# Attention-pack and channel mix on one core: first sequence's table and shares in long runs, v in two transfers, second sequence held, and a new order of all parts

## The chip, the cores and the metric

The kernel runs on one core of one Trainium2 chip. The metric is the device time in microseconds (us) of one execution. Several executions are timed, and their median is given; one further execution is profiled.

A core has TensorE (PE, matrix products), VectorE (DVE), ScalarE (ACT), GpSimd (POOL), and SyncE (SP), which here only starts transfers. DMA engines move data between device memory and on-chip memory; a transfer is started by an instruction on one engine's queue.

## The reference, cut to what matters

```python
def sm_attn(qq, kk, vv):                       # 8 sequences, 8 heads, 576 tokens, head size 64
    s = scale * np.matmul(qq, kk.transpose(0, 1, 3, 2))
    s = s - np.max(s, axis=-1, keepdims=True)
    a = np.exp(s)
    a = a / (np.sum(a, axis=-1, keepdims=True) + 1e-09)
    return np.matmul(a, vv)
p_packed = sm_attn(p, k, v)                    # p: 32 rows for each head
x = sm_attn(q, p_packed, p_packed)             # then heads side by side: 8 x 576 x 512

x_prev = shifted by one token within the sequence, zero ahead of the first
xk = mu_k * x + (1.0 - mu_k) * x_prev
xr = mu_r * x + (1.0 - mu_r) * x_prev
k = np.maximum(xk @ w_k, 0.0)                  # 512 -> 1024
v = k * k @ w_v                                # 1024 -> 512
r = 1.0 / (1.0 + np.exp(-(xr @ w_r)))          # the gates, 512 -> 512
out = r * v
```

## The kernel before, in words

**The two halves.** The attention half is called a front; there is one per sequence (b = 0 to 7). It multiplies k by p (L441 for the first sequence, L601 for the others), takes a softmax over the tokens, turns the weights (L687, L688), multiplies them by v (L462 or L623), and so has the packed rows. Then q meets the packed rows (L496 or L749), a second softmax over 32 follows, and the packed rows are mixed (L839 in the first sequence, where the mixing by mu_k, mu_r and the shift by one token are folded into the product with the shares `mub`; L796 and the DVE and ACT lines L916 to L936 in the others).

The first sequence's front is special: it goes in two sides, h = 0 and h = 1, of four heads each, and each step has its instructions once per side (`first_side`).

The second half works on 9 blocks of 512 tokens of all sequences side by side: gates (xr by w_r, L998 to L1000 for the first block, L1020 to L1022 later), keys (xk by w_k, L953 to L955, squared on ACT and DVE) and values (squared keys by w_v, L1049 to L1051). Each weight is held as a high and a low part in a reduced format, so each product of the second half is three matmuls. The last four blocks are computed in pairs with fewer products (L1353).

**The weights.** `convert` makes the two parts of each 128 x 512 piece of a weight from 64-bit numbers: a transfer into `st`, one ACT instruction (L344, `m` from one half of `st`), one shift on DVE (L350), one DVE instruction that joins in the other half (L352), a cast on ACT to the high part (L356) and a subtraction on DVE (L358). It has a second way, `by_act`, in which ACT runs one more instruction in place and DVE one in place of two; a piece takes it while fewer than RANK_LATE13 pieces have been begun. With 0.991 none does.

**The order.** `Flow` is a planner that runs when the program is built. All work is written as parts (generators), each with a rank; a part names its engine and its estimated time, waits for events, and takes and gives back buffer slots. The planner keeps a clock for each engine and always issues the instruction that can start first, ties broken by rank. What it issues is the fixed program order on each engine. On the chip the engines then run that order and wait for each other by semaphores; the planner's times play no part there. Where its clock shows TensorE idle, it issues `fill` (L1681): a product of the identity with itself that nothing reads. `fronts` starts the two sides of sequence 0 and then the other fronts one after the other.

**The first transfers.** SP starts k, v, q and the weights. p of the first sequence and the shares by channel (`mus`) go by ACT's queue, and the shares `mub` of the first sequence by POOL's:

```python
for hh, half in enumerate(HALVES):
    yield from load(pt[half, :, hh], p[0, half].rearrange("p (r n) -> p r n", n=NP), 0.5, 0.1, "scalar")
```

`pt` is cleared by POOL first; the two transfers write runs of 32 numbers (128 bytes). `mub` is spread over 64 partitions by 8 transfers of 64 x 128 numbers. v of one half sequence comes by one transfer of 512 KB (runs of 4 KB) and one small one.

Of the kernel before, what the change touches and what calls it, by code (L numbers as in the profile page):

```python
# [17 lines left out]
class Flow:  # L18
# [13 lines left out]
    URGENT = 10.6  # L32
# [158 lines left out]
def attn_pack_channel_mix(ctx: ExitStack, tc: tile.TileContext, q, k, v, p, mu_k, mu_r, mu_by_channel, w_k, w_v, w_r, out):  # L191
# [22 lines left out]
    FIRST = 19.125, 23.858, 15.496, 14.378  # L214
    RANK_1, RANK_MIX, RANK_KEYS, RANK_R, RANK_W, RANK_W2, RANK_V, LOADS_1, RANK_SQ, RANK_REST, HOLD_V, HOLD_S = 14.138, 6.204, 10.067, 22.577, 16.168, 18.235, 23.505, 24.159, 0.05, -0.644, 0.056, 0.212
    RANK_LATE1 = -1.892
    RANK_LATE2 = 4.895
    RANK_LATE3 = 0.077
    RANK_LATE4 = 7.126
    RANK_LATE5 = 4.101  # L220
    RANK_LATE6 = 1.945
    RANK_LATE13 = 0.991
    RANK_LATE12 = 22
# [29 lines left out]
    LANDS = 2.0  # L253
    MARGIN = 0.8
# [3 lines left out]
    def reached():  # L258
# [13 lines left out]
                pa=2, both=1, m=4, n=4, staged=4, ex=3, pair=0, ring=0, store=2, twin=0)  # L272
# [48 lines left out]
    def convert(w, hi, lo, c, o, n, event, first=None):  # L321
# [7 lines left out]
        yield from load(st[:, :2 * n], w[c * P:(c + 1) * P, o:o + n].bitcast(U32), 0.46, 3.5e-3 * n)  # L329
# [41 lines left out]
    def turned(src, tag, b, pr):  # L371

        slot = yield from flow.take("kq")
        t = tile_([P, S], F32, "kq", slot, tag)
        yield from load(t, src[b, pr], 0.46, 1.0)
        ts[tag, b, pr] = slot, t
        flow.set((tag, b, pr))
# [22 lines left out]
    def values_of(b, h):  # L400
# [7 lines left out]
        yield from load(vt[HALVES[h] if b >= MOVED else HALVES[0], 4], rest, 0.46, 0.3)  # L408
# [11 lines left out]
    def first_packed():  # L420
# [123 lines left out]
    def first_constants():  # L544
# [14 lines left out]
        for h in range(2):  # L559
            t = tile_([P, 4, P], F32, "sig", firsts["mu", h], "mub")  # L560
# [1187 lines left out]
```

## Time and profile before

| | before |
|---|---|
| timed runs, us | 561.14, 563.05, 563.52; median 563.05 |
| profiled execution, us | 561.01 |
| its span in the trace, us | 558.9 |
| TensorE busy | 550.4 us, 98% of the span |
| VectorE busy | 430.1 us, 77% |
| ScalarE busy | 349.0 us, 62% |
| moved by DMA | 86.10 MB, mean 154 GB/s |

The span is what the trace covers; 2.1 us of the profiled execution lie around it. TensorE's busy time includes the fills (L1681), so 98% doesn't say that 98% is work. A matmul's own duration overlaps the next one's: where the stream is dense, 512-column matmuls last about 0.39 us each and start about 0.227 us apart. So stretches are measured from start to start here.

### The profile page before, as it was taken

The numbers are of one execution on the slowest core, as the hardware profiler recorded it, in microseconds if no ns is written. First come the engines' busy times: TensorE is split into PE (matmuls) and PEld (weight loads), VectorE is DVE, ScalarE is ACT, GpSimd is POOL, SyncE is SP. The second block draws the span as 40 slices with busy tenths as digits, with TensorE's granted clock in tenths as the row PEclk, the third lists the DMA queues.
The fourth block names the chain that finished last, engine by engine and source line by source line (L and its number), as shares of the span: only waits on it lengthen the run. The fifth ranks groups of instructions, "written<-read, shape, count | busy, mean of one in ns | idle before, by whom it ended". The sixth has DMA issues, their size and how long they took to land.

```text
span 558.9 us, 9836 instructions
## 1 busy us (share of the span) xinstructions
PE 550.4 (98%) x3623; PEld 430.5 (77%) x3623; DVE 430.1 (77%) x857; ACT 349.0 (62%) x664; POOL 7.2 (1%) x36
## 2 busy tenths in 40 slices
PE   7999999999999999999999999999999999999997
PEld 6865787777777777777777877788888888888885
DVE  1788896878798599876798589924399894879863
ACT  2467776666675279356565468747797647877650
POOL 4000000000000000000000000000000000000000
PEclk9999999999999999999999999999999999999999
DMA  8985943445736563674614420220361480634242
GB/s 265 401 276 167 362 136 99 155 139 164 226 110 220 173 230 93 210 257 140 209 61 179 133 95 1 79 73 1 103 198 42 148 263 1 199 103 149 65 145 94
DMA packets 57135, 86.10 MB, mean 154 GB/s; under 512 B 6272, under 2 KB 33024, under 8 KB 57088
## 3 DMA queue, kind: packets, MB, share of 16 engines
q1 hardware_dynamic: 55424, 84.17, 45.4%
q10 hardware_dynamic: 1408, 1.05, 0.6%
q8 instruction: 28, 0.46, 0.3%
q0 software_dynamic: 256, 0.26, 0.2%
q14 instruction: 19, 0.16, 0.1%
HBM read 62.00 MB, written 23.46 MB: 153 GB/s over the span
## 4 chain that ended last, share of the span: by engine, by line
PE 83%; DVE 11%; ACT 2%; issue 2%; DMA 1%; DVEq 0%; ACTq 0%
PE ph L1353 31%; PE pvo L1049 6%; PE ph L953 6%; PE pvo L1050 5%; PE pvo L1051 5%; PE ph L954 5%; PE ph L955 5%; PE pr L1020 3%; PE pr L1021 3%; PE pr L1022 3%; PE pa L796 2%; PE pa L623 1%; DVE m L352 1%; PE pr L1509 1%; PE pr L1511 1%
## 5 line engine op out<-in xcount | busy, mean ns | idle before, releaser
L953 PE MATMUL ph<-xk,wk_h 128*128 128x512 f32 x160 | 64.1, 401 | 0.0
L1049 PE MATMUL pvo<-wv_h,sq 128*128 128x512 f32 x160 | 63.9, 399 | 0.2 <-ACT r L965 0.2
L954 PE MATMUL ph<-xk,wk_h 128*128 128x512 f32 x160 | 62.4, 390 | 0.0
L1050 PE MATMUL pvo<-wv_l,sq 128*128 128x512 f32 x160 | 62.4, 390 | 0.0
L955 PE MATMUL ph<-xk,wk_l 128*128 128x512 f32 x160 | 62.3, 389 | 0.0
L1051 PE MATMUL pvo<-wv_h,sq 128*128 128x512 f32 x160 | 62.2, 389 | 0.0
L965 ACT ACTIVATE r<-ph 128x512 f32<-128x512 f32 x40 | 23.9, 598 | 39.5 <-PE ph L955 29.8
L1353 PE MATMUL ph<-vT,ring 128*128 128x512 f32 x156 | 38.7, 393 | 0.0
L1049 PEld LDWEIGHTS pvo<-wv_h,sq 128*128 128x128 f32 x160 | 30.0, 188 | 11.3 <-issue 4.5
L953 PEld LDWEIGHTS ph<-xk,wk_h 128*128 128x128 f32 x160 | 30.0, 188 | 10.5 <-issue 4.1
L920 DVE SCALAR_TENSOR_TENSOR x<-xt,mus,x 128x64 f32<-128x64 f32 (+5 forms) x80 | 34.9, 480 | 4.1 <-ACT x L916 4.1
L916 ACT ACTIVATE x<-xt,mus 128x64 f32<-128x64 f32 (+5 forms) x80 | 35.8, 501 | 3.1 <-DVE xr L936 1.2
L955 PEld LDWEIGHTS ph<-xk,wk_l 128*128 128x128 f32 x160 | 30.0, 188 | 6.4
L1051 PEld LDWEIGHTS pvo<-wv_h,sq 128*128 128x128 f32 x160 | 30.0, 188 | 6.4
L1353 PE MATMUL ph<-vB,wv_h 128*128 128x512 f32 x112 | 34.8, 392 | 0.0
L1050 PEld LDWEIGHTS pvo<-wv_l,sq 128*128 128x128 f32 x160 | 30.1, 188 | 5.7
L954 PEld LDWEIGHTS ph<-xk,wk_h 128*128 128x128 f32 x160 | 30.1, 188 | 5.7
L1353 PEld LDWEIGHTS ph<-vT,ring 128*128 128x128 f32 x156 | 29.3, 188 | 6.6
L920 DVE SCALAR_TENSOR_TENSOR chain<-xt,mus,chain 128x448 f32<-128x448 f32 (+6 forms) x40 | 20.4, 535 | 17.3 <-ACT chain L916 17.1
L1031 ACT ACTIVATE sig<-pr 128x512 f32<-128x512 f32 x28 | 16.4, 600 | 21.5 <-PE pr L1022 11.3
L972 DVE CAST sq<-r 128x512 fp32r<-128x512 f32 x40 | 16.6, 417 | 16.2 <-ACT r L968 15.3
L974 DVE TENSOR_TENSOR sq<-r,sq 128x512 fp32r<-128x512 f32 x40 | 27.2, 683 | 0.2
(209 smaller groups left out, 1301.5 us busy)
## 6 DMA issues: line engine op xcount, KB each, us to landing
sum<-sw SPq DMA_DIRECT2D x40, 256.0 KB, 2.3
kT<-in_k SPq DMA_DIRECT2D x32, 288.0 KB, 4.5
qT<-in_q SPq DMA_DIRECT2D x32, 288.0 KB, 4.9
ring<-sum SPq DMA_DIRECT2D x36, 256.0 KB, 3.8
vt<-in_v SPq DMA_DIRECT2D x16, 512.0 KB, 5.7
out<-sig SPq DMA_DIRECT2D x32, 256.0 KB, 3.5
wv_h<-sum SPq DMA_DIRECT2D x18, 256.0 KB, 3.4
wv_l<-sum SPq DMA_DIRECT2D x18, 256.0 KB, 3.9
```

What stands on the lines that cost most here:

```text
L916: nc.scalar.mul(x32[:, o:o + n], xts[b, c][:, 1 + s:1 + s + n], mus[:, j, c:c + 1])
L920: nc.vector.scalar_tensor_tensor(x32[:, o:o + n], xts[b, c][:, s:s + n], mus[:, j + 1, c:c + 1], x32[:, o:o + n], op0=ALU.mult, op1=ALU.add,)
L953: nc.tensor.matmul(ph, wk_h[:, c, fs], xh, start=(c == 0), stop=False)
L954: nc.tensor.matmul(ph, wk_h[:, c, fs], xl, start=False, stop=False)
L955: nc.tensor.matmul(ph, wk_l[:, c, fs], xh, start=False, stop=(c == NC - 1))
L965: nc.scalar.activation(r, ph, AF.Relu)
L974: nc.vector.tensor_tensor(hl[:, 1, :], r, hl[:, 0, :].bitcast(F32), op=ALU.subtract)
L1020: nc.tensor.matmul(pr, xh[:, ts_], wr_h[:, c, :], start=(c == 0), stop=False)
L1049: nc.tensor.matmul(pv[t], sh, wv_h[:, f, :], start=(n == 0), stop=False)
L1050: nc.tensor.matmul(pv[t], sh, wv_l[:, f, :], start=False, stop=False)
L1051: nc.tensor.matmul(pv[t], sl, wv_h[:, f, :], start=False, stop=(n == NF - 1))
L1353: nc.tensor.matmul(bank[2], w, x, start=(not more and step == k == 0), stop=(step == 2 and k == count - 1), skip_group_check=True,)
```

## The change: what it does

1. p of sequence 0 is laid out on the host with its zeros (`p_first`), and comes in one transfer with runs of 1 KB on ACT's queue. POOL's clearing of `pt` goes.
2. The shares of the first sequence are spread over the partitions on the host (`mu_first`), and come in two transfers with runs of 1 KB on ACT's queue. The 8 POOL transfers go. `mus` comes in one transfer in place of two, and is now the first on ACT's queue.
3. The large part of v comes in two transfers with runs of 2 KB in place of one with runs of 4 KB, for every half sequence (16 more transfers on SP).
4. `fronts` waits until both sides of sequence 0 are mixed before it begins sequence 1.
5. All ranks, the planner's estimates for transfers, and two of its limits are new. RANK_LATE13 is 8.231, so the first 8 weight pieces take the way `by_act`.

Line numbers move: L441 to L529 stay; in what follows L839 is now L835, L687 is L683, L601 is L597, L998 is L994, L953 is L949, L1681 is L1675.

```diff
-    FIRST = 19.125, 23.858, 15.496, 14.378
...
-    RANK_LATE13 = 0.991
-    RANK_LATE12 = 22
+    FIRST = 8.643, 12.628, 9.429, 21.798
...
+    RANK_LATE13 = 8.231
+    RANK_LATE12 = 0.668
...
-        begin = max(flow.free.get("dma", 0.0), flow.t + 0.46)
+        begin = max(flow.free.get("dma", 0.0), flow.t + 0.46, SLOW[0])
+        if begin < SLOW[1]:
+            us *= SLOW[2]
...
+    SLOW = 1.2, 8.0, 1.3
...
-        yield from load(vt[:, :4], main, 0.46, 1.8)
-        back_to_issue()
+        for c in range(0, 4, 2):
+            yield from load(vt[:, c:c + 2], main[:, c:c + 2], 0.46, 0.65)
+            back_to_issue()
...
-        nc.gpsimd.memset(pt, 0.0)
-        for hh, half in enumerate(HALVES):
-            yield from load(pt[half, :, hh], p[0, half].rearrange("p (r n) -> p r n", n=NP), 0.5, 0.1, "scalar")
-            if not hh:
-                back_to_issue("scalar")
+        yield from load(pt, p_first.rearrange("p (r a n) -> p r a n", a=2, n=NP), 0.5, 0.25, "scalar")
...
-            t = tile_([P, 4, P], F32, "sig", firsts["mu", h], "mub")
-            for j, mu in ((2, mu_r), (0, mu_k)):
-                for c in range(2):
-                    at = (2 * h + c) * P
-                    yield from load(
-                        t[64 * c:64 * c + 64, j], mu[at:at + P].unsqueeze(0).broadcast_to([64, P]), 1.0, 0.02, "gpsimd"
-                    )
-                    back_to_issue("gpsimd")
+            t = tile_([P, 2, 2, P], F32, "sig", firsts["mu", h], "mub")
+            yield from load(t[:, 0], mu_first[:, h], 0.5, 0.3, "scalar")
+            back_to_issue("scalar")
...
         flow.spawn(rest_of_first(), RANK_REST)
+        yield from flow.wait(*(("mixed", h, tag) for h in range(2) for tag in ("xr", "xk")))
         for b in range(1, B):
...
-        for j in range(2):
-            yield from load(mus[:, 2 * j], mu_by_channel[:, j], 0.46, 0.02, "scalar")
-            if not j:
-                back_to_issue("scalar")
+        yield from load(mus[:, 0::2], mu_by_channel, 0.46, 0.02, "scalar")
```

**Three places in the order.** The first is TensorE at the start of the program, before the change:

```order
L1681 MATMUL spare<-ident 128x128 x12
L441 MATMUL pa<-kT,pt 64x288 x4
L1681 MATMUL spare<-ident 128x128 x10
L687 MATMUL pa<-ident,a 128x128 x4
L688 MATMUL pa<-ident,a 64x128
L1681 MATMUL spare<-ident 128x128 x5
L462 MATMUL pv<-vt,aT 32x64 x20
L1681 MATMUL spare<-ident 128x128 x2
L483 MATMUL pT<-ident,pm 128x128
L441 MATMUL pa<-kT,pt 64x288 x4
L496 MATMUL pa<-both,qT 128x64 x10
```

The same place after the change:

```order
L1675 MATMUL spare<-ident 128x128 x12
L441 MATMUL pa<-kT,pt 64x288 x4
L1675 MATMUL spare<-ident 128x128 x3
L441 MATMUL pa<-kT,pt 64x288 x4
L1675 MATMUL spare<-ident 128x128
L683 MATMUL pa<-ident,a 128x128 x4
L684 MATMUL pa<-ident,a 64x128
L1675 MATMUL spare<-ident 128x128 x5
L462 MATMUL pv<-vt,aT 32x64 x20
L683 MATMUL pa<-ident,a 128x128 x4
L684 MATMUL pa<-ident,a 64x128
L483 MATMUL pT<-ident,pm 128x128
```

The second L441, of side h = 1, stood behind the whole first softmax of h = 0 and its product with v; it now stands 3 fills behind the first L441. The 12 fills at the very start stay. In the whole program there are 62 fills before and 45 after.

The second place is TensorE around the first gates (L998 and L994), before the change, from the mixing of side h = 0 to the scores of sequence 1:

```order
L529 MATMUL pa<-ident,e 128x128
L1681 MATMUL spare<-ident 128x128 x9
L839 MATMUL pa<-a2t,mub 128x512 x4
L1681 MATMUL spare<-ident 128x128 x8
L998 MATMUL pr<-wr_h,xr 128x512
L999 MATMUL pr<-wr_l,xr 128x512
L1000 MATMUL pr<-wr_h,xr 128x512
L601 MATMUL pa<-kT,pt 32x288 x16
```

After the change:

```order
L1675 MATMUL spare<-ident 128x128 x4
L835 MATMUL pa<-a2t,mub 128x512 x4
L1675 MATMUL spare<-ident 128x128 x6
L529 MATMUL pa<-ident,e 128x112 x4
L529 MATMUL pa<-ident,e 128x128
L994 MATMUL pr<-wr_h,xr 128x512
L995 MATMUL pr<-wr_l,xr 128x512
L996 MATMUL pr<-wr_h,xr 128x512
L1675 MATMUL spare<-ident 128x128
L835 MATMUL pa<-a2t,mub 128x512 x4
L994 MATMUL pr<-wr_h,xr 128x512
```

Side h = 1 is turned (L529) ahead of the first gate, and its mixing (L835) comes directly behind it. Before, L529 of h = 1 stood behind 15 gate matmuls, and its L839 behind that. L601 of sequence 1 stood behind the first 3 gate matmuls; as L597 it now stands behind 27, with 21 left before the keys. Sequence 1's L687 (twice), L623, L653 and L749, which stood among the gates, stand as L683, L619, L649 and L745 among the keys of the first block: the first L683 is behind 30 key matmuls.

The third place is ACT around the first weight pieces, before the change (`a` and `e` belong to the softmaxes, `st`, `m` and `wr_h` to `convert`):

```order
L674 ACTIVATE a,sm<-pa,nmx 128x576
L514 ACTIVATE e<-e 128x640
L344 ACTIVATE m<-st 128x512 x2
L486 COPY both<-pT 128x128
L344 ACTIVATE m<-st 128x512
L356 CAST wr_h<-m 128x512
L344 ACTIVATE m<-st 128x512
```

After the change:

```order
L670 ACTIVATE a,sm<-pa,nmx 128x576
L345 ACTIVATE st<-st 128x512
L347 ACTIVATE m<-st 128x512
L486 COPY both<-pT 128x128
L345 ACTIVATE st<-st 128x512
L359 CAST wr_h<-m 128x512
L347 ACTIVATE m<-st 128x512
L514 ACTIVATE e<-e 128x640
L486 COPY both<-pT 128x128
```

L345 is the new ACT instruction, once for each of the first 8 pieces (4 of w_r, 4 of w_k). On DVE the shift (L350 before, L353 after) falls from 20 to 12, and the joining instruction stays at 20. Two pieces are now begun ahead of the second softmax of side h = 0 (L514).

## Rows read from the trace of the kernel before

**Rows 1.** Stretches: length; busy (instructions) PE, PEld, DVE, ACT, POOL; clock; DMA share; GB/s.

```profile
0.00:20.00 20.00, 16.66 (x151) 14.77 (x152) 4.68 (x13) 4.15 (x9) 6.07 (x25) 1.00 0.90 300
20.00:40.00 20.00, 19.88 (x198) 16.27 (x196) 19.12 (x40) 12.31 (x25) 0.00 (x0) 1.00 0.91 334
40.00:60.00 20.00, 18.98 (x187) 11.34 (x187) 15.30 (x30) 16.10 (x33) 0.10 (x1) 1.00 0.60 203
60.00:80.00 20.00, 20.00 (x116) 15.87 (x115) 19.45 (x39) 14.83 (x25) 0.00 (x0) 1.00 0.62 223
...
380.00:400.00 20.00, 20.00 (x89) 16.45 (x88) 10.36 (x18) 17.06 (x33) 0.00 (x0) 1.00 0.08 23
```

**Rows 2.** Timeline of TensorE, 0 to 33 us; at the end idle time before.

```profile
1.59 5.14 PE L1681 MATMUL spare<-ident 128*128 128x128 f32 x24 [1.59 <-POOL ident masks.py:199]
8.48 1.19 PE L441 MATMUL pa<-kT,pt 128*64 128x288 f32 x8 [1.75 <-DMA qT<-in_q]
9.60 2.50 PE L1681 MATMUL spare<-ident 128*128 128x128 f32 x20
...
15.40 1.19 PE L441 MATMUL pa<-kT,pt 128*64 128x288 f32 x8
16.52 2.44 PE L496 MATMUL pa<-both,qT 128*128 128x64 f32 x20
...
23.96 2.44 PE L496 MATMUL pa<-both,qT 128*128 128x64 f32 x20
...
28.84 1.99 PE L839 MATMUL pa<-a2t,mub 64*128 64x512 f32 x8
...
32.57 0.47 PE L998 MATMUL pr<-wr_h,xr 128*128 128x512 f32 x1
```

**Rows 3.** DMA issues of the first 25 us: KB each, median us to landing.

```profile
kT<-in_k SPq DMA_DIRECT2D x8, 288.0 KB, 5.1
...
pt<-in_p ACTq DMA_DIRECT2D x2, 32.0 KB, 6.1
```

**Rows 4.** Groups by line and form, 9 to 60 us: busy us, mean ns.

```profile
L344 ACT ACTIVATE m<-st 128x512 f32<-128x512 f32 x14 | 9.1, 686 | 0.0
...
L350 DVE TENSOR_SCALAR m<-m 128x512 uint32<-128x512 uint32 x13 | 5.4, 414 | 0.5 <-ACT m L344 0.5
L475 DVE SCALAR_TENSOR_TENSOR pm<-pv,rs,both 128x128 f32<-128x128 f32 x2 | 0.7, 348 | 2.8 <-PE pv L462 2.8
L699 DVE COPY aT<-pa 128x512 f32<-128x512 f32 x1 | 0.7, 680 | 0.0
```

**Rows 5.** Timeline of TensorE, 33 to 59 us.

```profile
33.44 1.35 PE L601 MATMUL pa<-kT,pt 64*32 64x288 f32 x32
...
38.26 0.66 PE L529 MATMUL pa<-ident,e 112*128 112x112 f32 x5
...
39.84 0.66 PE L687 MATMUL pa<-ident,a 128*128 128x128 f32 x4
...
40.54 3.70 PE L839 MATMUL pa<-a2t,mub 64*128 64x512 f32 x16
...
45.66 1.99 PE L839 MATMUL pa<-a2t,mub 64*128 64x512 f32 x8 [0.52 <-DVE xr L852]
...
51.21 1.48 PE L623 MATMUL pa<-vt,aT 128*32 128x64 f32 x80 [0.48 <-DVE xk L852]
...
56.61 1.20 PE L749 MATMUL pa<-qT,ppT 64*32 64x288 f32 x32
...
58.54 0.40 PE L953 MATMUL ph<-xk,wk_h 128*128 128x512 f32 x1
```

**Rows 6.** Timeline of TensorE, 93 to 108 us, around the second block's first gate (L1020).

```profile
93.36 0.74 PE L796 MATMUL pa<-a,pm 32*64 32x288 f32 x16
...
107.24 0.39 PE L1020 MATMUL pr<-wr_h,xr 128*128 128x512 f32 x1
```

**Rows 7.** Timeline of VectorE at the same place.

```profile
107.19 0.68 DVE L936 TENSOR_TENSOR xr<-x,xr 128x512 fp32r<-128x512 f32 x1
```

More of the change, by code (lines that the diff above doesn't have):

```diff
@@ L31 @@
     HOLD = {}
-    URGENT = 10.6
+    URGENT = 21.126
     CHANGE = 0.1
@@ L190, in attn_pack_channel_mix @@
 @with_exitstack
-def attn_pack_channel_mix(ctx: ExitStack, tc: tile.TileContext, q, k, v, p, mu_k, mu_r, mu_by_channel, w_k, w_v, w_r, out):
+def attn_pack_channel_mix(ctx: ExitStack, tc: tile.TileContext, q, k, v, p, p_first, mu_first, mu_by_channel, w_k, w_v, w_r, out):
     nc = tc.nc
@@ L211, in attn_pack_channel_mix @@
     flow = Flow()
-    FIRST = 19.125, 23.858, 15.496, 14.378
[L215 to L221, printed above, removed]
-    RANK_LATE13 = 0.991
-    RANK_LATE12 = 22
+    FIRST = 8.643, 12.628, 9.429, 21.798
+    RANK_1, RANK_MIX, RANK_KEYS, RANK_R, RANK_W, RANK_W2, RANK_V, LOADS_1, RANK_SQ, RANK_REST, HOLD_V, HOLD_S = 29.742, 22.85, 24.95, 30, 25.349, 24.645, 30, 29.932, 0.818, -6.71, 0.315, 0.438
+    RANK_LATE1 = -1.079
+    RANK_LATE2 = 0.189
+    RANK_LATE3 = 1.091
+    RANK_LATE4 = 9.432
+    RANK_LATE5 = 9.05
+    RANK_LATE6 = 20.949
+    RANK_LATE13 = 8.231
+    RANK_LATE12 = 0.668
     FIRST_K, FIRST_V, FIRST_Q = (RANK_LATE1, RANK_LATE2), (RANK_LATE3, RANK_LATE4), (RANK_LATE5, RANK_LATE6)
@@ L328, in convert @@
         st = tile_([P, 2 * WP], U32, "sq", slot, "st")
-        yield from load(st[:, :2 * n], w[c * P:(c + 1) * P, o:o + n].bitcast(U32), 0.46, 3.5e-3 * n)
+        yield from load(st[:, :2 * n], w[c * P:(c + 1) * P, o:o + n].bitcast(U32), 0.46, 2.45e-3 * n)
         flow.now.rank = rank
@@ L374, in turned @@
         t = tile_([P, S], F32, "kq", slot, tag)
-        yield from load(t, src[b, pr], 0.46, 1.0)
+        yield from load(t, src[b, pr], 0.46, 0.7)
         ts[tag, b, pr] = slot, t
@@ L724, in weights_moved @@
         away = dram.tile([P, NTB, NP], F32, name="away", tag=f"away{h}")
-        yield from load(away, blocks, 0.5, 0.9)
+        yield from load(away, blocks, 0.46, 0.8)
         flow.give("e", se)
@@ L839, in mixed_on_pe @@
                 nc.tensor.matmul(
-                    px[:, c, :TB], shares_of[half, j + t, :], a2[half, h, 1 - t:1 - t + TB], start=(t == 0), stop=(t == 1),
+                    px[:, c, :TB], shares_of[half, t, j // 2, :], a2[half, h, 1 - t:1 - t + TB], start=(t == 0), stop=(t == 1),
                 )
@@ L1062, in done @@
         t0 = i * TB + t * P
-        yield from load(out[t0:t0 + P, :], sig, 0.63, 0.75)
+        yield from load(out[t0:t0 + P, :], sig, 0.46, 0.65)
         flow.give("sig", sg)
@@ L1191, in stored @@
             yield from reached()
-            yield from load(dst, both, 0.5, 0.9)
+            yield from load(dst, both, 0.46, 0.65)
             flow.give("tmp", slot)
@@ L1250, in arriving @@
         for h, half in enumerate(both):
-            yield from load(half.bitcast(F32), sums[kind, SUM_OF[n], k][:, :, h], 0.5, 0.9)
+            yield from load(half.bitcast(F32), sums[kind, SUM_OF[n], k][:, :, h], 0.46, 0.65)
             if not h:
@@ L1592, in out_of_pair @@
         queue = "scalar" if i == PAIRS[-1] and n in (7, 4) else "queue"
-        yield from load(out[b * TB + d * P:b * TB + (d + 1) * P, :], sig, 0.46, 0.9, queue)
+        yield from load(out[b * TB + d * P:b * TB + (d + 1) * P, :], sig, 0.46, 0.65, queue)
         flow.give("sig", sg)
@@ L1716, in laid_out @@
     x['v'] = np.stack(by_half, axis=1)
-    x['mu_by_channel'] = np.stack([x['moe_mu_k'].reshape(-1, 128).T, x['moe_mu_r'].reshape(-1, 128).T], axis=1)
+    mus = np.stack([x['moe_mu_k'], x['moe_mu_r']]).reshape(2, -1, 128)
+    x['mu_by_channel'] = mus.transpose(2, 0, 1)
+    by_heads = mus.reshape(2, 2, 2, 1, 128).transpose(2, 3, 1, 0, 4)
+    x['mu_first'] = np.broadcast_to(by_heads, (2, 64, 2, 2, 128)).reshape(128, 2, 2, 128)
+    first = np.zeros((2, D, H // 2, 2, n), x['p'].dtype)
+    for h in range(2):
+        first[h, :, :, h] = x['p'][0].reshape(2, D, H // 2, n)[h]
+    x['p_first'] = first.reshape(2 * D, H * n)
     return x
```

15 lines of the change are left out of this document (8 added, 7 removed).

## The prediction

> **What bounds the kernel now.** I read the stretches first, because the busy shares of the whole span hide that the stages have different limits. In a late stretch (380 to 400 us) TensorE is busy all 20.00 us with 89 matmuls, one each 0.225 us: it is the bound, and DVE (10.36) and ACT (17.06) follow it [rows 1]. From 60 us on the stretches look like this one. Ahead of it they don't: to 20 us DVE and ACT are busy under 5 us each while DMA is at 0.90, and between 20 and 40 us DVE is busy 19.12 of 20 [rows 1]. TensorE's busy time there is partly fills and long gaps between products that matter.
>
> Next the timeline of TensorE shows what those first stages wait for. The first real product, L441 of side h = 0, starts at 8.48 behind a named wait of 1.75 us for a transfer [rows 2]. Side h = 1 has its L441 only at 15.40, and its L496 at 23.96, 7.44 behind that of h = 0 [rows 2]. The first gate is at 32.57, 24.1 us after the first L441. The keys begin at 58.54 [rows 5], 25.97 us after the first gate, and from there TensorE's dense stream runs to the end. So this change is worth what it moves the keys' start, less what it moves behind that start, plus what it makes late later.
>
> **The change part by part.**
>
> *p and the first product.* The two transfers of p take a median of 6.1 us from issue to landing although they hold 32 KB each; a kT of 288 KB takes 5.1 [rows 3]. So p's time is not bytes, and 128 runs of 1 KB in place of 512 of 128 bytes should bring it nearer to the kT's, or below. Bounds: no gain, 0; and the most that the fills allow. The 12 fills are 24 rows of the trace, from 1.59 for 5.14 us, and they end at 6.73 [rows 2]; L441 stands behind them in the new order too, and POOL's clearing of `pt`, gone now, stood ahead of the identity that they need, so they may end some tenths sooner. I take 6.4 as the earliest start of L441; the gain is 0 to 2.1. p is now issued behind `mus` on ACT's queue, one issue later than before, so I don't take the whole: **−1.8**, L441 at 6.7.
>
> *From the first L441 to the first gate, 24.1 us before.* In the new order L441 of h = 1 (1.19 us long [rows 2]) no longer stands between the softmax of h = 0 and its L496: −1.1. Between the reductions of the second softmax of h = 0 (L509 to L522), DVE ran a copy of 0.680, two shifts of 0.414 and L475 of 0.348 [rows 4], 1.86 us, and three small ones, some 2.4 in all; now it runs L475, two small ones and one subtraction on 512 columns, as long as the copy, some 1.3 in all: −1.1. The first gate needs this side alone. A further 0.4 is that fewer shifts stand between the mixing L839 and the gate. Sum **−2.6**, first gate at 28.2; bounds −1 (DVE's other work was in its gaps) and −4 (the h = 1 side doesn't collide at all).
>
> *From the first gate to the keys, 25.97 us before.* What TensorE has to do there is now 48 gate matmuls at 0.227, 10.9; L835 three more times at 1.85 to 1.99 [rows 5], 5.8; L597, 1.35 [rows 5]; L864, a product of 65 columns, 0.7 as I estimate it from L529's 0.66 [rows 5]; together 18.8, and 1.4 for changes between kinds of product and one wait as the two of 0.52 and 0.48 at 45.66 and 51.21 [rows 5]: 20.2, keys at 48.4. That is 10.1 earlier than 58.54. But sequence 1's L687 (twice 0.66), L623 (1.48), L749 (1.20) [rows 5], 4.0 in all, only moved behind the keys' start. TensorE's gain at an equal amount of work is therefore 10.1 − 4.0 = 6.1: the 1.8 and 2.6 above and **−1.7** here. Here the bounds are 0 and −2.8: waits as long as before, or none. What used to stall (mixing of h = 1 behind DVE's and ACT's conversions) finds DVE freer: the shifts of 8 pieces, 8 x 0.414 = 3.3 [rows 4], are gone from it.
>
> *by_act.* Those 8 pieces cost ACT 8 x 0.686 = 5.5 us more [rows 4], all in the first 50 us. ACT is busy 12.31 and 16.10 of 20 there [rows 1], so 5.5 fits the sum, but most of what it has free is ahead of 40 us. What waits behind it is the exponential of sequence 1, without which L683 holds TensorE's queue among the keys, and the squares' first step of the keys. Bounds 0 and 3 (half of 5.5); **+0.8**.
>
> *Second sequence held.* L601 was at 33.44, L597 stands 7 gate groups ahead of the keys, at about 42.2. The path from there to the second block's gates was 73.8 us (33.44 to L1020 at 107.24 [rows 5, 6]), and will be 60.7. At the end of it nothing was spare: xr's last subtraction on DVE is at 107.19 and L1020 at 107.24 [rows 6, 7] (it needs that xr only for its last steps). From L796 at 93.36 to this the chain takes 13.8 [rows 6, 7], and the order leaves it about 14.6. Work fits: some 80 DVE instructions lie in the window, at the 0.50 of 60:80 (19.45 for 39 [rows 1]) 40 us of 60.7. **+0.5**, 0 to 1.
>
> *The order of transfers.* kT of h = 1 now comes ahead of the first v, as do shares and two weight pieces ahead of q of h = 1. Up to the q that the second L496 needs, SP's and ACT's orders hold 5.5 MB. Before, 6.0 MB were moved by 20.00 us (300 GB/s [rows 1]), so 5.5 are there at about 18.5 and landed some tenths to 2 us later; I have that L496 at 19.9. **+0.6**, 0 to 1.2. v in halves: 16 more issues on SP, which only issues, and whose transfers from 40 us on leave DMA at a share of 0.60 and less [rows 1]: 0, and if that cover were gone, some 0.5 each time that v is the last to land.
>
> **Sum:** −1.8 − 2.6 − 1.7 + 0.8 + 0.5 + 0.6 = −4.2. The profiled execution took 561.01 (span 558.9 and 2.1 around it), so 556.8. The three timed runs' median stands 2.0 above the profiled one, so the same change would be 558.8 on it; I give **557.5**, between. The bounds together reach from about 552 (−2.1 − 4 − 2.8) to the old time.
>
> *A rule against it.* To 6.7 us TensorE's fills pass at 5.14/24 = 0.214 us each, from 9.60 at 2.50/20 = 0.125 [rows 2]: by that pace TensorE starts at the lower of its two clock levels (1.2 of 2.4 GHz), and had risen after it was kept busy, though the column of the granted clock says 1.00 throughout [rows 1]. The Trainium skill, "TensorE: Matmul & The Clock Gate", section "HAM oscillation — how this bites in real kernels", says that idle gaps put TensorE back to the lower level, so that each next batch starts cold; 45 fills in place of 62 leave more such gaps. By the rows the sum stands as above. By the rule, one fall between 7 and 28 us would double the short products that follow until it has risen, about the 4.6 us of a side's L441, L496 and L687 at half pace, and cost 2.3 more: 559.8. No stretch here shows TensorE slower again once it had risen, with gaps of the same kind among its products [rows 1, 2], so I give it 0.05.
>
> **The rivals.**
>
> *A. Transfers hold it (0.12).* DMA is at 0.90 of its share to 20 us [rows 1], and the same bytes come in. If q and w_r pieces are what h = 1 and the gates wait for, the second and third term shrink to about −1 each, and +1.2 stands for the order: −2.6, about **559.5**. For it: the share. Against it: DVE is busy 19.12 of 20 between 20 and 40 us, with data there [rows 1].
>
> *B. ACT becomes the limit in the first keys (0.14).* The extra 5.5 us come out at the exponential of sequence 1, TensorE stops at L683, and squares come late for the values. Then +3, and with a first product that gains only 1: −1.2, about **561.8**, no change that can be told. For it: 16.10 of 20 already busy in 40:60 [rows 1].
>
> *C. The second sequence is held too long (0.09), slower than before.* DVE's 40 us and the tail of 13.8, taken one behind the other, are 53.8 of the 60.7 us from L597 to L1020, so 6.9 are left for waits between the chain's steps; before, with 73.8, they took 20. As soon as they take over 6.9, TensorE has no other work at L1020 and stops, us by us; if they take three quarters of the old 20, 15, it waits 8, and the time is **565.5**. For it: nothing was spare at 107.24 [rows 6, 7]. Against it: L601 was begun early, and most of the 20 lay where its chain had time.
>
> *D. More than I sum (0.10).* No term later, the first ones near their bounds: **552.5**.
>
> **How the numbers follow.** The forecast has 0.50, the rule 0.05, A 0.12, B 0.14, C 0.09, D 0.10. Within 0.5% (2.8 us, about what a measurement here can tell from no change) of 563.05 lie B and a part of A's and the forecast's upper end. Faster by over 0.5%: 0.73; within: 0.18; slower: 0.09. The range is 552 to 562: it leaves out C and the ends of B and D. The forecast's own range is 555 to 560.
>
> **What would show it.** L441 at 6.4 to 7.5 and its second one right behind; the second L496 within 6 us of the first; the first gate at 27 to 29.5, the first key at 47 to 50; among the first keys no idle time of TensorE ahead of L683 above 1 us; L1020 at 102 to 104.5 with DVE's xr just ahead. A late landing of p or of a first v behind `mus`, an idle TensorE ahead of L683, or ahead of L1020, would make it wrong, each by the size of that gap.

## The result, and the profile after

The changed kernel takes 556.01 us (median of 554.85, 555.34, 556.68, 557.18) against 563.17 for the kernel before, beside which it ran; the ratio is 0.988, with a 95% interval of 0.985 to 0.991. That is faster by about 7 us. 557.5 was predicted, with a range of 552 to 562.

The profiled executions differ by less than the medians (7.16 us): 554.85 against 561.01, which is 6.16, and spans of 553.3 against 558.9, which is 5.6. The 0.55 between these two is time outside the span: 2.1 us before and 1.5 after. What makes that differ isn't shown; it lies between 1.5 and 2.2 in all runs below. So there are two things to find: where the trace's 5.6 come from, and what the medians have beyond them.

The timeline of TensorE after the change, rows that answer to [rows 2], [rows 5] and [rows 6]:

```profile
1.48 5.03 PE L1675 MATMUL spare<-ident 128*128 128x128 f32 x24 [1.48 <-POOL ident masks.py:199]
6.43 1.19 PE L441 MATMUL pa<-kT,pt 128*64 128x288 f32 x8
8.42 1.19 PE L441 MATMUL pa<-kT,pt 128*64 128x288 f32 x8
14.04 2.44 PE L496 MATMUL pa<-both,qT 128*128 128x64 f32 x20
19.59 2.44 PE L496 MATMUL pa<-both,qT 128*128 128x64 f32 x20
23.90 1.99 PE L835 MATMUL pa<-a2t,mub 64*128 64x512 f32 x8
27.67 0.48 PE L994 MATMUL pr<-wr_h,xr 128*128 128x512 f32 x1
...
41.83 1.20 PE L597 MATMUL pa<-kT,pt 64*32 64x288 f32 x32
47.90 0.39 PE L949 MATMUL ph<-xk,wk_h 128*128 128x512 f32 x1
55.96 0.65 PE L683 MATMUL pa<-ident,a 128*128 128x128 f32 x4 [1.10 <-ACT a L670]
101.69 0.40 PE L1016 MATMUL pr<-wr_h,xr 128*128 128x512 f32 x1
```

The reader can lay these starts beside those of before and take differences. L441 is at 6.43 for 8.48 (−2.05). From there to the first gate it is 21.24 us for 24.09 (−2.85), from the gate to the first key 20.23 for 25.97. Of these last 5.74, 4.0 are the work of sequence 1 that moved behind the key, so −1.74. At the key the gain is 6.64. From the key to the second block's gate it is 53.79 for 48.70, 4.0 of which are that work: 1.1 lost, and the row of L683 names it, an idle time of 1.10 ahead of it until ACT's exponential. The gain at L1020, now L1016, is 5.55, and at the end 5.6: behind 102 us the change neither gained nor lost on balance.

The −2.85 between L441 and the first gate are not one thing. These rows of DVE, TensorE and ACT, first before and then after, part them:

```profile
9.72 0.76 DVE L668 TENSOR_REDUCE mx<-pa 128x1 f32<-128x576 f32 x1 [9.72 <-PE pa L441]
19.00 0.82 DVE L509 TENSOR_REDUCE m<-pa 128x20 f32<-128x640 f32 x1 [1.39 <-PE pa L496]
23.42 0.81 DVE L522 TENSOR_TENSOR e<-e,m 128x640 f32<-128x640 f32 x1
26.24 0.67 PE L529 MATMUL pa<-ident,e 112*128 112x112 f32 x5
26.74 2.17 PE L1681 MATMUL spare<-ident 128*128 128x128 f32 x18
27.37 0.27 ACT L536 COPY a2t<-pa 128x128 f32<-128x128 f32 x1
```

```profile
7.96 0.29 DVE L568 TENSOR_SCALAR mub<-mub 128x256 f32<-128x256 f32 x1 [3.75 <-DMA mub<-in_mu_first]
8.17 0.75 DVE L664 TENSOR_REDUCE mx<-pa 128x1 f32<-128x576 f32 x1
16.52 0.83 DVE L509 TENSOR_REDUCE m<-pa 128x20 f32<-128x640 f32 x1 [0.83 <-PE pa L496]
20.62 0.83 DVE L522 TENSOR_TENSOR e<-e,m 128x640 f32<-128x640 f32 x1
22.37 0.66 PE L529 MATMUL pa<-ident,e 112*128 112x112 f32 x5
22.87 1.05 PE L1675 MATMUL spare<-ident 128*128 128x128 f32 x8
23.50 0.27 ACT L536 COPY a2t<-pa 128x128 f32<-128x128 f32 x1
```

- From L441 to the first reduction on DVE (L668, now L664) it is 1.74 us for 1.24, 0.50 lost: the new order puts L568 ahead of that reduction, and L568 waits for the first shares.
- From that reduction to the first L496 it is 5.87 for 6.80, −0.93: L441 of side h = 1 is out of the way.
- From L509 to L522, the second softmax on DVE, it is 4.10 for 4.42, −0.32.
- From L522 to L529 it is 1.75 for 2.82, −1.07. L529 stands on TensorE behind the L496 of h = 1. That one started at 23.96 before, when e was nearly done, and starts at 19.59 now, ahead of L522.
- From L529 to the mixing it is 1.53 for 2.60, −1.07. What the mixing needs of L529 was copied by ACT at 27.64 before (L536), but L839 started only at 28.84, behind 9 fills (18 rows). Now the copy ends at 23.77, only 4 fills stand there, and L835 starts at 23.90.
- From the mixing to the first gate it is 3.77 for 3.73.

Of the transfers of the first 25 us, the row of p, which answers to [rows 3]:

```profile
pt<-in_p_first ACTq DMA_DIRECT2D x1, 128.0 KB, 3.4
```

p has four times the bytes of each of the two short-run transfers, and takes 3.4 us to land where they took 5.8 and 6.4 (median 6.1).

ACT's timeline ahead of L683:

```profile
52.50 0.59 ACT L961 ACTIVATE r<-ph 128x512 f32<-128x512 f32 x1
53.12 0.64 ACT L964 ACTIVATE r<-r 128x512 f32<-128x512 f32 x1
53.78 1.28 ACT L670 ACT_TABLE_LOAD   x1
55.07 0.74 ACT L670 ACTIVATE a<-pa,nmx 128x576 f32<-128x576 f32 x1
```

The exponential stands behind the key's first steps and a table load, and TensorE waits for it.

### The profile page after: what moved, and what is told of

Its sections match the earlier page's. It is cut to its first block, busy times and chain, and to the rows that moved or that the text cites. A ratio compares the mean times of both kernels' runs of the same rounds, so it can differ in the third digit from the quotient of the medians.

```text
span 553.3 us, 9754 instructions
## 1 busy us (share of the span) xinstructions
PE 546.5 (99%) x3589; PEld 426.4 (77%) x3589; DVE 432.5 (78%) x849; ACT 356.6 (64%) x672; POOL 2.7 (0%) x27
## 4 chain that ended last, share of the span: by engine, by line
PE 91%; DVE 3%; ACT 2%; DMA 2%; issue 1%; ACTq 0%; DVEq 0%
PE ph L1349 31%; PE pvo L1045 7%; PE ph L949 7%; PE pvo L1046 7%; PE pvo L1047 7%; PE ph L950 6%; PE ph L951 6%; PE pr L1016 3%; PE pr L1018 3%; PE pr L1017 3%; PE pa L792 2%; PE pa L619 2%; PE pa L745 1%; PE pr L1506 1%; PE pr L1505 1%; PE pr L1507 1%
## 5 line engine op out<-in xcount | busy, mean ns | idle before, releaser
L949 PE MATMUL ph<-xk,wk_h 128*128 128x512 f32 x160 | 64.5, 403 | 0.0
L949 PEld LDWEIGHTS ph<-xk,wk_h 128*128 128x128 f32 x160 | 30.0, 188 | 11.6 <-issue 5.4
L1349 PE MATMUL ph<-vT,ring 128*128 128x512 f32 x150 | 37.2, 393 | 0.0
L916 DVE SCALAR_TENSOR_TENSOR chain<-xt,mus,chain 128x448 f32<-128x448 f32 (+6 forms) x40 | 20.3, 536 | 17.3 <-ACT chain L912 17.3
L1349 PE MATMUL ph<-vB,wv_h 128*128 128x512 f32 x100 | 31.3, 394 | 0.0
L1349 PE MATMUL ph<-vT,wv_h 128*128 128x512 f32 x92 | 28.7, 393 | 0.0
```

The source lines that it names most:

```text
L916: nc.vector.scalar_tensor_tensor(x32[:, o:o + n], xts[b, c][:, s:s + n], mus[:, j + 1, c:c + 1], x32[:, o:o + n], op0=ALU.mult, op1=ALU.add,)
L949: nc.tensor.matmul(ph, wk_h[:, c, fs], xh, start=(c == 0), stop=False)
L1349: nc.tensor.matmul(bank[2], w, x, start=(not more and step == k == 0), stop=(step == 2 and k == count - 1), skip_group_check=True,)
```

## The experiments

Each kernel ran beside the kernel before on the same chip. The four executions of the changed kernel alone spread over 2.3 us, so a median is uncertain by about 1 us, and the stages of the trace are read too. The edits are cut to their main lines, and comments in them stand for what is left out. Starts of a stage are written as L441 / first gate / first key / second block's gate; before it is 8.48 / 32.57 / 58.54 / 107.24, after 6.43 / 27.67 / 47.90 / 101.69.

**1. The order alone.** After's order, before's transfers of p, shares and mus.

```diff
-        yield from load(pt, p_first.rearrange("p (r a n) -> p r a n", a=2, n=NP), 0.5, 0.25, "scalar")
+        yield from load(pt, None, 0.5, 0.25, "scalar", in_short_runs)   # clears pt; p in two, mus in two
...
-            yield from load(t[:, 0], mu_first[:, h], 0.5, 0.3, "scalar")
+            yield from load(t[:, 0], None, 0.5, 0.3, "scalar", by_pool) # the 8 transfers of before
```

> The changed kernel with its whole order, but p, the shares and mus come as before the change (p in two transfers of 128-byte runs behind POOL's clearing, mus in two behind it, the shares in 8 POOL transfers). Theory of the prediction (the start and the order add up): L441 waits for p again and starts at 8.3 to 8.9, DVE's first reduction stands behind the first shares at 9.4 to 9.8 instead of 8.17, and all that follows is 1.3 to 1.8 us later than in the changed kernel: first gate at about 29.2, first key at about 49.5, time about 1.5 us above the changed kernel (ratio to before about 0.991). Rival 1 (w_r and q are what the gates wait for): first key within 0.4 us of 47.9 and the time that of the changed kernel. Rival 2 (the transfers are what pays, the order nothing): first key past 52 and the time within 1 us of before.

Measured: 557.98 (ratio 0.992, 0.989 to 0.995), 2.0 above the changed kernel; 8.01 / 29.08 / 51.22 / 105.19. The start and the gate came as the theory has them (+1.58 and +1.41), the key later than it has it (+3.32). TensorE waited 1.85 ahead of L835 (here line 855), and behind that stood a weight transfer:

```profile
37.98 1.99 PE L855 MATMUL pa<-a2t,mub 64*128 64x512 f32 x8 [1.85 <-DVE xr L868]
34.73 0.67 ACT L348 ACTIVATE st<-st 128x512 uint32<-128x512 uint32 x1 [1.97 <-DMA st<-in_moe_w_k]
35.30 0.56 ACT L866 CAST xr<-pa 128x512 fp32r<-128x512 f32 x1
```

xr's cast queues behind a conversion whose w_k piece has not landed. The profiled execution is the slowest of its four by 0.9, so its key is also on the late side. Rivals 1 and 2 fall: the transfers are worth 1.4 to 1.6 at the start and the gate, and the order alone pays 5.3 against the median of before. All four executions here have a mean granted clock of 0.999 or 1.000; against the three of before with 1.000 (see 2) the order pays 3.5 to 4.0.

**2. The transfers alone.** Before's order, after's transfers of p, shares and mus.

```diff
-            yield from load(pt[half, :, hh], p[0, half].rearrange("p (r n) -> p r n", n=NP), 0.5, 0.1, "scalar")
+            yield from load(None, None, 0.5, 0.1, "scalar", in_one)     # mus in one, then p_first in one
...
-                    yield from load(t[64 * c:64 * c + 64, j], mu[at:at + P]..., 1.0, 0.02, "gpsimd")
+                    yield from load(None, None, 1.0, 0.02, "gpsimd", all_first)  # mu_first on ACT's queue
```

> The kernel before with its whole order, but p, the shares and mus come as in the change (three kinds of transfer on ACT's queue, no clearing, no POOL transfers; v stays in one). Theory of the prediction: L441 starts at 6.3 to 6.8 and the path of side h = 0 follows, first gate 1.2 to 2.0 us ahead of 32.57 and first key as much ahead of 58.54, so the time is 1.2 to 2.0 us below before (ratio about 0.997). Rival 1 (the gain is hidden): L441 is earlier, but the first gate stays within 0.4 us of 32.57, because w_r's pieces, landed at 17 to 22 us before, and DVE's conversions of them set it; ratio 1.000. Rival 2 (the transfers are most of the whole gain): first key at 54 or earlier, ratio 0.991 or less.

Measured: 559.61 (ratio 0.993, 0.991 to 0.996), 3.6 below before; 7.01 / 31.10 / 57.08 / 105.80. All stages follow the 1.47 of L441, within 0.03, as the theory says, and rivals 1 and 2 fall. But the median fell by 2 us more than the stages did. This was the first sign of something that the trace of before doesn't show: all 7 executions here have a mean granted clock of 0.999 or 1.000, and of the 16 executions of before beside them only 3 have 1.000 (561.5 to 562.0 us); the other 13 have 0.993 to 0.997 and take 562.7 to 564.8. (The expectation of experiment 8 says 12 and 4; 13 and 3 is right.)

**3. v in one transfer.**

```diff
-            yield from load(vt[:, c:c + 2], main[:, c:c + 2], 0.46, 0.65)
+            yield from load(None, None, 0.46, 0.65, "queue", (lambda: nc.sync.dma_start(vt[:, :4], main)) if not c else lambda: None)
```

> The changed kernel in the same order, but the large part of v comes in one transfer of 512 KB again, for every half sequence. Theory of the prediction: nothing, the first v lands by 10.5 us where L462 needs it at 11.9, and later v lie ahead of their use; stages within 0.3 us of the changed kernel's, ratio to it 0.998 to 1.002. Rival (halves let the queue of transfers move earlier): first v lands past 11.5, L462 waits for it, and the first key is 0.5 us or more later, the time 0.5 to 1.5 us above.

Measured: 555.85 (ratio 0.988, 0.985 to 0.991); 6.74 / 27.81 / 47.95 / 102.34. Nothing, as expected; its wait ahead of L683 was 1.7 in place of 1.1, which is the 0.6 at the last stage.

**4. No fills behind the first 12.**

```diff
+        filled.append(1)
+        if len(filled) <= 12:
             nc.tensor.matmul(spare[:, :P], ident, ident, start=True, stop=True)
```

> The changed kernel in the same order without the 33 fills behind the first 12, so that TensorE is idle wherever it waits between 7 and 29 us. Theory of the prediction (fills behind the start carry nothing): second L496 still at 19.6 and first gate at 27.7, each within 0.3 us, time as the changed kernel. Rival (the rule of the Trainium skill, TensorE: Matmul & The Clock Gate, section HAM oscillation, as weighed in the prediction: TensorE falls back to the lower clock level in gaps): short products last about twice as long from some point behind 7 us on, an L496 group 4 to 5 us instead of 2.4, first gate at 29.5 or later, and the first gate matmuls start 0.45 us apart instead of 0.23; time 2 us or more above the changed kernel.

Measured: 559.30 (ratio 0.994, 0.992 to 0.996), 3.3 above the changed kernel. All 10 executions have a mean granted clock of 0.982 to 0.994. The rival is right: without these fills the clock does fall. Stretches of this run (length; busy time with instructions of PE, PEld, DVE, ACT, POOL; clock; DMA share; GB/s), and its timeline:

```profile
15.00:20.00 5.00, 2.85 (x52) 2.12 (x50) 4.03 (x10) 3.72 (x7) 0.00 (x0) 0.89 1.05 389
20.00:25.00 5.00, 5.00 (x24) 4.69 (x23) 1.55 (x2) 1.21 (x2) 0.00 (x0) 0.50 1.04 384
```

```profile
18.19 0.33 PE L483 MATMUL pT<-ident,pm 128*128 128x128 f32 x1 [1.02 <-DVE pm L475]
19.47 4.77 PE L496 MATMUL pa<-both,qT 128*128 128x64 f32 x20 [0.94 <-DMA qT<-in_q]
26.10 3.48 PE L835 MATMUL pa<-a2t,mub 64*128 64x512 f32 x8 [0.91 <-DVE e L511]
```

TensorE was busy 2.85 of 5 us between 15 and 20, with two gaps of about 1 us, and then runs at the lower level (0.50 of 2.4 GHz is 1.2): the second L496 takes 4.77 for 2.44. Until 14 us this run was ahead (first L496 at 13.45, since no fill stands in the way); the first gate is at 30.26, 2.6 late. The Trainium skill, "TensorE: Matmul & The Clock Gate", section "HAM oscillation — how this bites in real kernels", says that idle gaps put TensorE back to the lower level; the trace of this run agrees, with 0.50 in 20:25. In the changed kernel, which keeps 33 fills in these gaps, all four executions show 0.999 or 1.000.

**5 and 6. No hold, and no by_act.** Both make the planner order everything behind them anew, with ranks that belong to the change.

```diff
-        yield from flow.wait(*(("mixed", h, tag) for h in range(2) for tag in ("xr", "xk")))
```

> The changed kernel without the wait of fronts for the mixing of sequence 0, all ranks kept; the planner then makes the order anew. In it L597 of sequence 1 and its two reductions on DVE stand ahead of the mixing of side h = 0, and L683, L619 and more of sequence 1 are back among the gates. Theory of the prediction (holding pays because DVE is the limit between 20 and 40 us): the first gate is 3 to 6 us later than 27.7, and at the second block's gates, where the same work is done in both, 2 to 4.5 us of it are left; time 2 to 4.5 above the changed kernel (558 to 560.5). Rival (the hold only moves work): second block's first gate within 1 us of 101.7, time within 1 us of the changed kernel.

```diff
-    RANK_LATE13 = 8.231
+    RANK_LATE13 = 0.991
```

> The changed kernel with RANK_LATE13 = 0.991, so that no weight piece takes by_act; the order is made anew behind the first gate (sequence 1's L683, L619, L649 and L745 stand among the gates again). Theory of the prediction (by_act relieves DVE and costs ACT): first gate within 0.5 us of 27.7; the stretch from it to the second block's first gate is longer by 0.5 to 2, DVE's 8 shifts (3.3 us) set against ACT's 5.5 and the wait ahead of L683 (1.1 us) that goes; time 0 to 1.5 above the changed kernel. Rival (ACT is the limit of the first keys, B of the prediction): without the 8 instructions the wait is gone and nothing new comes, second block's first gate at 100.8 or earlier, time 0.8 or more below the changed kernel.

Measured: without the hold 566.45 (ratio 1.006, 1.004 to 1.008); 5.70 / 36.64 / 63.87 / 115.25. The direction is the theory's, the size isn't: 9.0 at the first gate, where 3 to 6 were expected, and 13.6 at the second block's, where 2 to 4.5 were. Without by_act 570.15 (ratio 1.014, 1.010 to 1.017); first gate 28.02 as expected, second block's gate 118.99. Its largest wait of TensorE:

```profile
PE pa L683 <- ACT a L670: 7.2, 2, 7.1
```

Between 46 and 53 us ACT worked through conversions of w_k and w_v ahead of that exponential, waiting for pieces to land (0.93, 0.16, 0.59) and for DVE (1.05), while L683 stood among the gates. Neither theory nor rival said this. Nor is that wait all of the 17.3 us at the second block's gate: TensorE was busy 1.71 and 1.13 of 5 us in 45:50 and 50:55, and the granted clock was 0.60, 0.50 and 0.54 in the three stretches from 45 to 60 us and 0.66 in 35:40. All four executions here have a mean of 0.985 to 0.988, and the ten without the hold 0.994 to 0.997, so both runs also hold a loss by the clock that the change itself doesn't have. Both runs tell how little margin the planner's order has once one part of it is undone; what the hold or by_act are worth by themselves under ranks of their own they don't tell, and that stays open.

**7. L683 later.**

```diff
-        yield pe(0.65)
+        yield pe(0.65, flow.t + 1.3 if b == 1 else None)
```

> The changed kernel, planned with sequence 1's L683 1.3 us later, so that it stands two groups of three key matmuls further back. Theory 1 (the 1.10 us that TensorE waited ahead of L683 for ACT's exponential are lost time): the wait is 0.3 us or less, the second block's first gate is 0.7 to 1.2 us earlier than 101.7, and so is the time. Theory 2 (the chain of sequence 1 decides at the second block's gates, as C of the prediction has it, since its last xr on DVE ended at 104.2 just ahead of its matmul at 104.28): the wait ahead of L683 goes, but TensorE waits as much among those gates, and the time is within 0.4 us of the changed kernel.

Measured: 556.66 (ratio 0.989, 0.986 to 0.992); 6.72 / 27.68 / 47.91 / 102.86. The time is 0.65 above the changed kernel and the wait ahead of L683 fell to 0.25, but neither theory is right: the second block's first gate is 1.2 later than in the changed kernel, not earlier (theory 1), and TensorE does not wait among those gates (theory 2). From its waits in this run:

```profile
PE pa L619 <- ACT aT L700: 0.4, 1, 0.4
PE pa L745 <- ACT ppT L652: 0.3, 1, 0.3
...
PE pa L619 <- ACT aT L702: 0.3, 1, 0.3
PE pa L683 <- ACT a L670: 0.3, 1, 0.3
PE pa L649 <- DVE pm L643: 0.2, 1, 0.2
```

In place of one wait of 1.10 there are five among the later steps of sequence 1, 1.5 us together, 1.3 of them behind ACT. That is 0.4 of the 1.2; the rest lies in no wait that is listed, and stays open.

**8 and 9. More and fewer fills ahead of the first product, in the kernel before.**

```diff
+        filled.append(1)
+        for _ in range(4 if len(filled) == 12 else 1):
             nc.tensor.matmul(spare[:, :P], ident, ident, start=True, stop=True)
```

> The kernel before with 15 fills in place of 12 ahead of the first L441, nothing else. Before, TensorE is idle 1.75 us ahead of L441, and of 16 executions 12 show a mean granted clock of 0.993 to 0.997 and take 562.7 to 564.8 us, the 4 others 1.000 at 561.1 to 562.0. Theory (in most executions of before that gap lets the clock fall for a while; the change's earlier p closes it, and this is the part of its gain that the stages of the trace don't show): the idle time ahead of L441 is 0.7 us or less, L441 still starts at 8.3 to 8.7, all stages stay within 0.3 us of before, but nearly all executions show 0.999 or more, and the median falls to 560.8 to 561.8. Rival (the falls come from somewhere else): clocks of 0.993 to 0.997 in most executions again, median within 0.6 us of 563.2.

```diff
+        filled.append(1)
+        if len(filled) > 3:
             nc.tensor.matmul(spare[:, :P], ident, ident, start=True, stop=True)
```

> The kernel before with 9 fills in place of 12 ahead of the first L441, nothing else: the opposite of 15. Theory (the idle time ahead of L441 lets the clock fall): that idle time grows to about 3 us, L441 still starts at 8.3 to 8.7, every execution shows a mean granted clock of 0.997 or less and none takes under 562.3 us, the median lies at 563.3 to 565.5; the trace shows the lower level in a stretch behind L441, where an L496 group takes 4 to 5 us in place of 2.44 and the first gate comes 1 us or more later than 32.57. Rival (the falls come from elsewhere, or fewer fills only start the clock's rise later): clocks spread as before, 0.993 to 1.000, median within 0.6 us of 563.2.

Measured with 15: 561.51 (ratio 0.998, 0.996 to 0.9995); 8.68 / 32.77 / 58.74 / 107.47. Eleven of 12 executions have 0.999 or 1.000 (560.84 to 561.90), one 0.997 (563.63). All stages are 0.2 later than in the trace of before, and yet the median fell by 1.8 (by the ratio 1.2): this is the theory as it was put. The idle time ahead of L441 is down from 1.75:

```profile
8.68 1.19 PE L441 MATMUL pa<-kT,pt 128*64 128x288 f32 x8 [0.66 <-DMA qT<-in_q]
```

With 9: 563.87 (ratio 1.000, 0.998 to 1.001). The trace shows the fall where the theory has it:

```profile
5.00:10.00 5.00, 1.69 (x10) 1.10 (x11) 0.00 (x0) 0.00 (x0) 1.74 (x7) 0.86 0.94 300
10.00:15.00 5.00, 5.00 (x37) 4.13 (x34) 1.56 (x6) 1.29 (x3) 0.00 (x0) 0.80 0.90 277
```

```profile
8.88 2.19 PE L441 MATMUL pa<-kT,pt 128*64 128x288 f32 x8 [3.31 <-DMA pt<-in_p]
```

Behind an idle time of 3.31 the first product takes 2.19 for 1.19, and the first gate is at 34.43. But the L496 groups, which the expectation had at 4 to 5 us, take 2.45, and the median hardly moved. The clocks of the executions lie between 0.993 and 1.000, and five of them have 0.999 or 1.000, four of which still take 563.8 to 564.5. Why these are slow without a lower clock on record isn't shown. So 15 fills bear the theory out, and 9 do so in the one trace only.

**10. The kernel before, a second trace.**

> The kernel before, unchanged, for a second trace: three in four of its executions so far showed a mean granted clock of 0.993 to 0.997, and the trace that the prediction was read from is of one without. Theory: where the clock is below 0.999, the stretch of 5:10 or 10:15, around and behind the idle time ahead of L441, is the one with a granted clock well below 1.00, the fills or products there take about twice as long, and the first gate comes 1 us or more later than 32.57. Rival: the lower stretch lies elsewhere (the last 200 us, or the gaps between 40 and 58 us), and the first gate is within 0.4 us of 32.57. If the execution shows 1.000, it tells nothing.

Measured: 563.62, clock 0.995; 9.41 / 35.09 / 61.03 / 109.81. Stretches, and the timeline of TensorE:

```profile
5.00:10.00 5.00, 2.63 (x16) 2.28 (x17) 0.00 (x0) 0.00 (x0) 1.75 (x7) 1.00 0.94 276
10.00:15.00 5.00, 5.00 (x31) 4.37 (x28) 1.56 (x6) 0.83 (x2) 0.00 (x0) 0.66 0.94 335
15.00:20.00 5.00, 5.00 (x74) 3.85 (x72) 2.03 (x5) 1.01 (x3) 0.00 (x0) 1.00 0.96 356
```

```profile
9.41 1.38 PE L441 MATMUL pa<-kT,pt 128*64 128x288 f32 x8 [2.37 <-DMA pt<-in_p]
10.72 3.90 PE L1681 MATMUL spare<-ident 128*128 128x128 f32 x20
14.46 0.60 PE L687 MATMUL pa<-ident,a 128*128 128x128 f32 x4
```

p landed 0.9 later than in the first trace, TensorE idled 2.37 ahead of L441, the clock fell in 10:15 (0.66), and the 20 rows of fills behind L441 took 3.90 in place of 2.50. They now end past the softmax and hold L687. The first gate is 2.5 later than in the first trace [rows 2], and so is every stage to the end. Of these 2.5, 0.93 are p's later landing, there before the clock falls; 1.6 are the fall (from L441 to L687 it is 5.05; in the first trace, with L687 at 11.94, it is 3.46).

**11 and 12. The shares' counterparts later, and 8 fills with it, in the changed kernel.**

```diff
-        nc.vector.tensor_scalar(t[:, 1], t[:, 0], -1.0, 1.0, op0=ALU.mult, op1=ALU.add)   # in first_others
...
         yield vec(4 * P)
+        nc.vector.tensor_scalar(t[:, 1], t[:, 0], -1.0, 1.0, op0=ALU.mult, op1=ALU.add)   # in first_shares
```

> The changed kernel, in which DVE makes the shares' counterparts (L568, twice) directly ahead of L577, where they are used, in place of ahead of its first reduction, where it waited for the first shares until 7.93. Theory (that wait delays side h = 0 by what lies between the end of L441 and 8.17): first reduction at 7.6 to 7.9, first L496 0.2 to 0.5 us earlier than 14.04; side h = 1, whose kT landed at 8.22 and whose q landed at 19.27, gains nothing, so the first key stays within 0.3 us of 47.9 and the time within 0.5 us of the changed kernel. Rival (side h = 0 alone sets the keys): first key 0.4 us or more earlier.

For the 8 fills `fill` also leaves out the first 4 of its products (`if len(filled) > 4:`).

> The same, with 8 fills in place of 12 at the start. p landed at 4.87 in the changed kernel, so the fills alone held L441 to 6.43. Theory (behind the fills the transfers are next): L441 starts at 4.9 to 5.5, at the lower clock level, the first reduction at 6.5 to 7.5, but v (10.5) and q (12.84) hold L462 and the first L496 to 12.9 or later and q of h = 1 (19.27) the second L496 to 19.4 or later; first key within 0.5 us of 47.9, time 0 to 0.7 us below the changed kernel, if the clock doesn't fall. Rival 1 (the start is worth its whole 1.2 us): first key at 47.0 or earlier, time 0.8 us or more below. Rival 2 (the gaps let the clock fall): mean granted clock 0.997 or less, time 1 us or more above.

Measured: 556.07 (ratio 0.987, 0.985 to 0.989), 6.83 / 28.09 / 48.37 / 102.33; with 8 fills 556.50 (ratio 0.987, 0.985 to 0.990), 6.32 / 28.55 / 49.12 / 103.50. Neither is faster than the change. The first of them did not even move its first L496 (14.15), as L441 was 0.4 later in it, though from L441 to L496 it is 7.32 for 7.61. The first keys are 0.5 and 1.2 later than in the changed kernel, where 0.3 and 0.5 at most were expected. With 8 fills L441 was not at 5: p landed at 6.2 and TensorE waited 1.06 for it. Its first L496 is 0.4 earlier, its second waits twice:

```profile
19.78 0.41 PE L496 MATMUL pa<-both,qT 128*128 128x64 f32 x2 [0.50 <-DMA qT<-in_q]
20.38 2.22 PE L496 MATMUL pa<-both,qT 128*128 128x64 f32 x18 [0.19 <-DMA qT<-in_q]
```

So in this trace p is next behind the fills, and behind p it is q of h = 1; the rest of the lateness at the key isn't shown.

## Why the prediction was right

**The terms.** Predicted and measured in the trace: p and the first product −1.8 and −2.05; to the first gate −2.6 and −2.85; to the keys −1.7 and −1.74; ACT among the keys +0.8 and +1.1; second block's gates +0.5 and 0; order of transfers +0.6 and 0. The sum was −4.2 and is −5.55 at L1016. The start's part is shown by the pair of 1 and 2: each half of the change without the other moves L441 and the gate about as its own term says. The third term is right in its working too: 18.8 us of work and 1.4 around it were forecast between the first gate and the keys, 20.2, and it is 20.23.

The second term is right in its sum by luck. Its parts were −1.1 for side h = 1's L441, −1.1 for a freer DVE in the second softmax, and −0.4 behind the mixing. The trace has −0.93, −0.32 and +0.04 for these, 1.4 less than forecast. It has +0.50 for the wait for the shares, which the prediction did not have, and −2.14 for two things that it did not put into the sum: L529 waits less behind the L496 of h = 1, and 4 fills in place of 9 stand ahead of the mixing. So a freer DVE is a small part of it. These parts are read from two traces; no run parts them.

**The two terms that came to nothing.** At the second block's gates there is no idle time ahead of L1016. The matmul at 104.28 stands right behind DVE's xr (L932, 103.54 for 0.69), and starts 0.08 later than the pace of 0.23 would have it. And q of h = 1 landed at 19.27, just ahead of its L496 at 19.59, so the order of transfers cost nothing, with 0.3 us to spare; experiment 12 shows the cost as soon as one leans on it.

**The rule that I had on the wrong side.** I weighed the clock against the change, at 0.05, because no row of before showed a fall. The trace of before was of one of the few executions without one. In most of them the clock falls, and 8 and 10 show where: with three useless products more in the gap ahead of L441 the falls are nearly gone and the median is 1.8 us lower (1.2 by the ratio), and a trace with the fall has it behind that gap and loses 1.6 us by it. The changed kernel's executions all show 0.999 or 1.000, and its trace has no idle time ahead of L441. The new p is not needed for that: in experiment 1, with the old transfers in the new order, p lands at 7.88, TensorE idles 1.22 ahead of L441, and no execution shows a fall. Experiment 4 shows the rule against the change too, where the fills are taken away. The price that the prediction gave it, 2.3, was also too low by its own rows: L441, L496 and L687 take 4.3 us at the higher level [rows 2, 5], so half the pace adds about as much; in experiment 4 one L496 alone grew by 2.33.

**The number.** The medians' 7.16 are the traces' 5.6, the 0.55 outside the span, and 1.0 for where the medians stand: before, 2.16 above its profiled execution, as executions with and without a fall differ in 2; after, 1.16 above its own, without any. The 557.5 was 1.5 too high because the sum was short by 1.4 and lacked the 0.55, less 0.45, as 0.7 was allowed between profiled execution and median and 1.16 came. That it stands between the two bases of 556.8 and 558.8 has no reason in the prediction, which did not ask what the 2.0 between the timed runs and the trace were.

**The rivals.** A (transfers) has no term in the changed kernel, but is what made the profiled execution of experiment 1 late at the keys. B (ACT) is real, at 1.1 in place of 3, and 7 speaks for ACT's whole queue and not the place of one product. C did not come; L597 was at 41.83, as forecast (42.2), and nothing waited at L1016. D (552.5) overshot: the first term came to its bound (2.05 of 2.1), but the second and third stayed far from theirs. Two of the signs were missed by little: TensorE idled 1.10 ahead of L683, where at most 1 was given, and L1016 is at 101.69, where 102 to 104.5 was.

## What to carry to other kernels

Measure a change in the order of a start-up from start to start, stage by stage, and subtract work that only moved past the mark: the sum then meets the end of the trace to 0.1 us. Do the same within a term: a sum that fits can hide parts that don't. Look at the granted clock of every execution, not only of the profiled one, before calling a gap harmless; a cheap product that fills the gap tells whether the clock is in it. But fills ahead of a product that is ready hold it: 9 of them cost the first mixing of before 1.1 us. A part of an order that was tuned as a whole can't be priced by undoing it alone.

## What was not expected of the hardware

The same transfer of p, 128 KB in runs of 1 KB issued at 1.48, landed at 4.87 in the changed kernel's trace, at 6.23 to 6.88 in those of experiments 2, 3 and 4, at 5.08 to 5.63 in those of 5, 6 and 7, and at 6.18 and 6.21 in those of 11 and 12. So it moves by 2 us between traces, which is more than most terms of the sum. Each of these groups ran on a chip of its own, so whether the chip, the execution or the order makes it isn't shown.

The 12 fills at the start took 4.29 us in the trace of experiment 5 and 5.42 in that of 11, and L441 stood right behind them, at 5.70 and 6.83:

```profile
1.48 4.29 PE L1674 MATMUL spare<-ident 128*128 128x128 f32 x24 [1.48 <-POOL ident masks.py:199]
1.48 5.42 PE L1675 MATMUL spare<-ident 128*128 128x128 f32 x24 [1.48 <-POOL ident masks.py:199]
```

Their rows start 0.21 us apart at first; in the one trace the last 10 steps are 0.11, in the other none is. So the clock's rise, earlier or later, moved the first product by 1.1 us with nothing changed ahead of it.

TensorE's mean clock of 0.995 over a span, which reads like nothing, was one stretch at 0.66 in 10:15, and cost 1.6 us because fills stood ahead of a product that mattered.
